# Reciprocals of softmax sums moved to ScalarE as exp(-ln), fewer k^T v bursts, and another eviction order at the first weight folds

## The chip, the cores and the metric

One core of one Trainium2 chip runs the kernel. Its engines are TensorE (PE in the profile, with its weight loads as PEld), VectorE (DVE), ScalarE (ACT), GpSimd (POOL) and SyncE (SP, which here only issues DMAs). The metric is the device time of one execution in microseconds; lower is better.

## The reference

A transformer block on x of 2048 rows and 640 columns: a linear attention with 32 heads of 20 columns, then a gated feed-forward network of width 1536. Inputs and output are bf16.

```python
x = A_x
h  = x + A(layernorm(x))
h2 = h + (gelu(ln(h) @ w_gate) * (ln(h) @ w_up)) @ w_down

# A: per head
pq, pk = q @ w_phi, k @ w_phi
phi_q = concat(softmax(pq), softmax(-pq))      # over 20 columns each
phi_k = concat(softmax(pk), softmax(-pk))
kv  = phi_k^T v ;  z = sum over rows of phi_k
o   = (phi_q kv) / (phi_q z + 1e-6)            # then @ wo
```

## The kernel before

The 2048 rows are 16 tiles of 128 rows (t = 0 to 15), with all 640 columns in the free dimension; four tiles make a block b. Nothing is left to a planner: `manual_schedule` keeps the order in which the code is written, on every engine's queue. So an instruction that waits holds all that is written behind it on the same engine.

**Folds.** w_phi is multiplied into the weights first: `fold` makes W_k w_phi and W_q w_phi in five chunks of 128 rows each. A chunk is a few matmuls into a PSUM tile `wa` (L248) and one eviction into Wk2 or Wq2, on ScalarE for the chunks listed in KA and QA (L257), else on VectorE (L259). The five W_k folds stand ahead of the main loop, the five W_q folds in its iterations 10 to 14 (FQ).

**Main loop, L494 to L534, t = 0 to 15.** One iteration does, in this order on each queue: the layernorm of tile t+6 on ScalarE (`ln_ap`, L151, up to t = 9; its transpose is a DMA that SP issues, L167); `k_tile(t)`: ten matmuls into `pk` (L296), then two exponentials on ScalarE, exp(pk) and exp(-pk), into E(t) (L340); a fold of W_q (t = 10 to 14); a burst of `kv_tile`s if KVG names t; at t = 15 the q products (`q_mm`, L396) and their exponentials (`q_exp`, L401) with the burst KVQ after the first group; `v_mm(t+3)` (L296) and its eviction `v_ev(t+3)` on ScalarE (L316) into the buffer vS of which there are NV; `k_norm(t)`.

**k_norm(t), L343.** VectorE sums E(t) over each head's 20 columns (`sk`, 64 sums a row, L347) and takes reciprocals (`rs`, L351). Then E(t) is multiplied by rs in place, in two halves (L355): the exp(-pk) half on GpSimd, the exp(pk) half on GpSimd too for the tiles in VP, else on VectorE, one iteration later (`todo`).

**k^T v bursts, L370.** `kv_tile(t)` is 32 small matmuls (L374), one for each head, with 32 columns of v as weights, all accumulating into one PSUM tile `kvp`. They run in bursts: tiles 0 and 1 in iteration 6, tiles 2 to 4 in iteration 9, tiles 5 to 8 in iteration 13, tiles 9 to 12 between q groups, tiles 13 to 15 after the loop. E has 10 buffers: E(t) overwrites E(t-10) once its `kv_tile` is done.

**PSUM.** Up to the middle of the feed-forward stage all PSUM tiles (`pk`, `pv`, `wa`, `tp`, `kvp`, `pq`) come from one pool, psG, of four buffers; a buffer is reused after its tile has been evicted. `kvp` keeps one from its first burst to the end of k^T v, and three rotate.

**After the loop**: `kv_mask` (VectorE), then attention and the feed-forward network, woven together from L831 on. None of that is touched.

Of the kernel before, what the change touches and what calls it, by code (L numbers as in the profile page):

```python
# [11 lines left out]
ACTF = mybir.ActivationFunctionType  # L12
# [5 lines left out]
def kernel(  # L18
# [12 lines left out]
    nc = tc.nc  # L31
    P = 128
    S = 2048
    D = 640
    H = 32
# [9 lines left out]
    H0 = [(P * c) // Dh for c in range(NC)]  # L45
    NH = [(P * c + P - 1) // Dh - H0[c] + 1 for c in range(NC)]
    VP = (0, 2, 4, 6, 7, 9, 11, 12)
    KA, QA = (0, 1, 4), (0, 1, 2, 3, 4)
    LQ = (7, 9, 9, 9, 10)
    FQ = (10, 11, 12, 13, 14)  # L50

    QG = ((5, 6), (0, 1), (2, 3), (4,), (7, 8), (9, 10), (11, 12), (13, 14), (15,), (16,), (17,), (18,), (19,))
    QT = (15, 15, 15, 15)
    T3 = 3

    KVG = {6: (0, 1), 9: (2, 3, 4), 13: (5, 6, 7, 8)}
    KVQ = {0: (9, 10, 11, 12)}
    VC = Dh + 1
    KC = Dh + 2
# [8 lines left out]
    SLOT = [(5 * (c // 2) + 2 * (c % 2), 3 * (c // 2) + c % 2, 2 + c % 2) for c in range(NC)]  # L68
    SL = 12
    DC = 512 - 9 * KC  # L70
    NV = 11

    x_v = A_x.rearrange("b (p t) d -> p (b t) d", t=NT)
    o_v = out.rearrange("b (p t) d -> p (b t) d", t=NT)
# [33 lines left out]
    def small(pool, shape, name, bufs=3):  # L108
        return pool.tile(shape, F32, name=name, bufs=bufs)

    def gtile(name):
        return psG.tile([P, 2, 512], F32, name=name, tag="G")
# [62 lines left out]
    p1 = p1_cm.__enter__()  # L175
    Wv = p1.tile([P, NC, D], BF16, name="Wv")
    Wk2 = p1.tile([P, NC, D], BF16, name="Wk2")

    vF = [p1.tile([P, H * VC + 11], BF16, name=f"vS{i}") for i in range(NV)]
    vS = [v[:, 0:H * VC].rearrange("p (h f) -> p h f", f=VC) for v in vF]  # L180
# [19 lines left out]
    def load_T(WT, i, *ds):  # L200

        for d in ds:
            nc.sync.dma_start_transpose(WT[:, :, d * P:(d + 1) * P], A_wqkv[d * P:(d + 1) * P, i * D:(i + 1) * D])  # L203
# [7 lines left out]
    ones = nc.const_aps.tensor(1.0, [P, 512], BF16)  # L211
    for i in range(NV):
        nc.vector.memset(vS[i][:, :, 0], 1.0)
    make_identity(nc, ident)
    nc.gpsimd.memset(hmask, 1.0)
    for c in range(NC):
# [4 lines left out]
                                compare_op=ALU.is_ge, fill=0.0, base=Dh - 1 - off, channel_multiplier=-1)  # L221
    for i in range(NV):
        nc.gpsimd.memset(vF[i][:, H * VC:], 1.0)
# [8 lines left out]
    def fold(WT, W2, quarters, ds=range(NC)):  # L232


        n, w = (2, QF) if quarters else (1, HD)
        runs = []
        for c in range(NC):
            lo, hi = H0[c] * Dh, (H0[c] + NH[c]) * Dh
            for r in range(2 * n):
                a, b = max(lo, r * w), min(hi, (r + 1) * w)  # L240
                if a < b:
                    runs.append((r // n, r, c, a, b))
        runs.sort()
        for d in ds:
            wa = gtile("wa")
            wr = wa.rearrange("p u (q x) -> p (u q) x", q=n)
            for i, (u, r, c, a, b) in enumerate(runs):
                nc.tensor.matmul(wr[:, r, a - r * w:b - r * w], lhsT=WT[:, c, d * P:(d + 1) * P],  # L248
                                 rhs=BD[:, c].rearrange("p a b -> p (a b)")[:, a - H0[c] * Dh:b - H0[c] * Dh],
                                 start=(i == 0 or runs[i - 1][0] != u),  # L250
                                 stop=(i + 1 == len(runs) or runs[i + 1][0] != u), skip_group_check=True)
            dst, src = W2[:, d, :].rearrange("p (u f) -> p u f", u=2), wr[:, :, 0:w]
            if quarters:
                dst = W2[:, d, :].rearrange("p (c r f) -> p r c f", c=NC, r=4)
                src = src.rearrange("p r (c f) -> p r c f", c=NC)
            if d in (QA if quarters else KA):
                nc.scalar.copy(dst, src)  # L257
            else:
                nc.vector.tensor_copy(dst, src)  # L259
# [19 lines left out]
    def ln_ap(t, on_act=False, on_pe=False):  # L279
        ln = (ln_act if on_act else ln_dve)(p1, "1", *lnp[t])  # L280
        if on_pe:
            lnp[t] = ln
        else:
            transpose_to(LN1T[t // 4][:, :, t % 4 * P:(t % 4 + 1) * P], ln, False)

    def ln_tp(t, on_dve=False):
        transpose_to(LN1T[t // 4][:, :, t % 4 * P:(t % 4 + 1) * P], lnp[t], True, on_dve)
# [5 lines left out]
    def proj(ps, t, W, us=(0, 1), cs=None):  # L293
        order = [(u, c) for u in us for c in range(NC)] if cs is None else [(u, c) for c in cs for u in us]
        for u, c in order:
            nc.tensor.matmul(ps[:, u, 0:HD], lhsT=lnT(t, c), rhs=W[:, c, u * HD:(u + 1) * HD],  # L296
                             start=(c == 0), stop=(c == NC - 1))
# [3 lines left out]
    def v_mm(t, us=(0, 1)):  # L301
        if 0 in us:
            pv[t] = gtile("pv")
        proj(pv[t], t, Wv, us)
# [10 lines left out]
    def v_ev(t):  # L315
        nc.scalar.activation(vS[t % NV][:, :, 1:VC].rearrange("p (u h) f -> p u h f", u=2),  # L316
                             pv[t][:, :, 0:HD].rearrange("p u (h f) -> p u h f", f=Dh), ACTF.Copy,
                             scale=lnp[t][2] if t in CT else 1.0)
# [7 lines left out]
    def k_part(t, *cs):  # L326
        if 0 in cs:
            pks[t] = gtile("pk")
        proj(pks[t], t, Wk2, cs=cs)

    def k_tile(t):
        if t in pks:
            pk = pks[t]
            k_part(t, NC - 1)
        else:
            pk = gtile("pk")
            proj(pk, t, Wk2)
        Ek[t] = ev.tile([P, 2, D], BF16, name="E", bufs=10)
        for s in range(2):
            nc.scalar.activation(Ek[t][:, s, :].rearrange("p (u f) -> p u f", u=2), pk[:, :, 0:HD],  # L340
                                 ACTF.Exp, scale=((lnp[t][2], nrstd[t]) if t in CT else (1.0, -1.0))[s])

    def k_norm(t):  # L343


        sk = small(p1, [P, 2 * H], "sk")
        nc.vector.reduce_sum(sk, Ek[t].rearrange("p s (h f) -> p (s h) f", f=Dh), axis=AX.X)  # L347
        if t - 1 in todo and t < NT - 1:
            todo.pop(t - 1)()
        rs = small(p1, [P, 2 * H], "rs")  # L350
        nc.vector.reciprocal(rs, sk)  # L351

        def mult(s, eng):
            e = Ek[t][:, s, :].rearrange("p (h f) -> p h f", f=Dh)
            eng.tensor_tensor(e, e, rs[:, s * H:(s + 1) * H, None].to_broadcast([P, H, Dh]), ALU.mult)  # L355

        mult(1, nc.gpsimd)
        if t in VP:
            mult(0, nc.gpsimd)
        elif t == NT - 1:  # L360
            todo.pop(t - 1)()
            mult(0, nc.vector)
        else:
            todo[t] = lambda: mult(0, nc.vector)

    todo = {}

    def kv_tile(t):

        E = Ek[t].rearrange("p s (h f) -> p s h f", f=Dh)  # L370
        for i in range(QH):
            for r in range(4):
                h = r * QH + i
                nc.tensor.matmul(kvp[QUAD[r], :, i * Dh:(i + 1) * Dh], lhsT=vF[t % NV][:, h * VC:h * VC + 32],  # L374
                                 rhs=E[:, :, h, :], start=(i == t == 0), stop=(t == NT - 1), skip_group_check=True)
# [23 lines left out]
    def q_exp(j, signs=(0, 1)):  # L399
        for s in signs:  # L400
            nc.scalar.activation(Eq[j][:, :, s, :], pqs[j][:, 0:len(QG[j])], ACTF.Exp, scale=(1.0, -1.0)[s])  # L401
# [66 lines left out]
    ln_st(4, act=False, between=lambda: ln_ap(3, on_pe=True))  # L468
    ln_tp(3, True)
    nc.sync.dma_start(x_sb[1][:, 2:4, :], x_v[:, 6:8, :])  # L470
    fold(WkT, Wk2, False, (0,))
    v_ev(2)
    fold(WkT, Wk2, False, (1,))
    ln_st(5, act=False, between=lambda: ln_ap(4))
    nc.sync.dma_start(x_sb[2][:, 0:2, :], x_v[:, 8:10, :])
# [18 lines left out]
    for t in range(NT):  # L494
        if t == T3:
            kvp = gtile("kvp")[:, 0, 0:2 * QF].rearrange("p (s f) -> p s f", s=2)
        late = t in (1, 4)
        if 0 < t < NT - 6 and not late:
            ln_ap(t + 6, on_act=True)
        k_tile(t)  # L500
        if t == 0:
            ln_ap(6)
            nc.sync.dma_start(x_sb[3][:, 0:2, :], x_v[:, 12:14, :])
        if t in FQ:
            fold(WqT, Wq2, True, [i for i, f in enumerate(FQ) if f == t])
        for i in KVG.get(t, ()):
            kv_tile(i)
        for j in range(len(QT)):
            if t == QT[j]:
                q_mm(j)  # L510
                q_exp(j)
                for i in KVQ.get(j, ()):
                    kv_tile(i)
        if 0 < t < NT - 3:
            v_mm(t + 3)
        if late:
            ln_ap(t + 6, on_act=True)
        if t == 1:
            nc.sync.dma_start(x_sb[3][:, 2:4, :], x_v[:, 14:16, :])
        if 0 < t < NT - 3:  # L520
            v_ev(t + 3)
        for i in ST.get(t, ()):
            ln_st(i, i + 1)
        k_norm(t)
        load_T(WqT, 0, *[i for i, f in enumerate(LQ) if f == t])
        if t == 10:
            transpose_to(LN1T[0][:, :, P:2 * P], ln_a(1), False)
        if t == 13:
            ln_ap(0, on_act=True)
        if t == 8:  # L530
            for z in KT:
                nc.gpsimd.memset(z, 0.0)
        if t == 13:
            nc.sync.dma_start(Wo, wo_v)  # L534
# [402 lines left out]
```

## Time and profile before

| | |
|---|---|
| Time, median of 3 runs | 272.33 us (272.25 to 272.48) |
| The profiled execution's own time | 272.0 us |
| Its span, first to last instruction | 270.3 us |
| Granted TensorE clock | 1.0 |
| Main loop's first burst of k^T v | 30.75 us |
| End of the last burst of k^T v | 67.1 us |
| Instructions of `sk`, mean | 16, 1.43 us each |
| Instructions of `rs`, mean | 16, 0.55 us each |

The profile is of one execution; what lies between its span and its time is start and end of the launch. In a timeline line the columns are start and duration in us, engine, source line, operation, output and inputs with their shapes, the number of instructions that the line merges, and in brackets the idle time of the engine before it with what ended it. In a group's line a bar is followed by busy time in us and the mean of one in ns, then by idle time before. Instructions of ScalarE and VectorE overlap a little at their ends, so a step from start to start is shorter than a duration.

### The profile page before, as it was taken

What the parts mean: (1) busy time and instruction counts of PE and PEld (TensorE: products, weight loads), DVE (VectorE), ACT (ScalarE), POOL (GpSimd) and SP (SyncE); (2) the same over time, 40 slices, a digit from 0 to 9 for tenths busy, and PEclk for the clock granted to TensorE, in tenths of its full rate; (3) what the DMA queues carried; (4) which work ended last, traced back from release to release, by engine and by line L of the source; (5) the groups of instructions that cost most, each with busy time, mean ns of one, the idle gap of its engine ahead of it and who ended that gap; (6) DMA issues with size and microseconds to landing.
All of it is one profiled execution on the core that took longest, in us unless ns stands there. A gap on an engine that the chain in (4) does not pass through costs nothing.

```text
span 270.3 us, 7032 instructions
## 1 busy us (share of the span) xinstructions
PE 265.5 (98%) x2851; PEld 171.7 (64%) x2867; DVE 176.4 (65%) x348; ACT 138.1 (51%) x248; POOL 99.5 (37%) x236
## 2 busy tenths in 40 slices
PE   8999999999999999999999999999999999999995
PEld 6777777764455887788755455775555476444574
DVE  5899999998876758876566783568663322333322
ACT  5769997887789675245541356321544300322100
POOL 5448988794002335376211664014561100000000
PEclk9999999999999999999999999999999999999999
DMA  7998255240678432332201224103222101000011
GB/s 192 213 203 175 54 86 100 62 127 26 233 260 232 155 101 62 41 98 51 52 24 51 49 50 51 49 2 78 78 41 52 24 24 51 24 0 0 4 49 49
DMA packets 45264, 22.10 MB, mean 82 GB/s; under 512 B 37808, under 2 KB 43184, under 8 KB 45232
## 3 DMA queue, kind: packets, MB, share of 16 engines
q1 hardware_dynamic: 44576, 21.64, 33.0%
q8 instruction: 22, 0.36, 0.6%
q10 hardware_dynamic: 656, 0.03, 0.2%
q14 instruction: 10, 0.08, 0.1%
HBM read 10.18 MB, written 2.62 MB: 47 GB/s over the span
## 4 chain that ended last, share of the span: by engine, by line
PE 87%; SPq 4%; DVE 2%; POOL 2%; DMA 2%; issue 1%; ACT 1%; ACTq 0%; POOLq 0%
PE gu L767 38%; PE pd L789 20%; PE po L707 8%; PE pq L396 8%; PE pk L296 5%; PE pv L296 4%; SPq L203 2%; PE kvp L374 2%; DMA x_sb<-in_A_x_dram 2%; PE ab L618 1%; POOL E L355 1%; DVE stats L121 1%; PE ab L585 1%; PE wa L248 1%; DVE sk L347 1%
## 5 line engine op out<-in xcount | busy, mean ns | idle before, releaser
L770 ACT ACTIVATE g<-gu 128x512 bf16<-128x512 f32 (+1 forms) x60 | 30.4, 510 | 74.0 <-PE gu L767 73.2
L773 DVE TENSOR_TENSOR GT<-gu,g 128x512 bf16<-128x512 f32 (+1 forms) x60 | 34.4, 580 | 46.6 <-PE gu L767 38.8
L767 PE MATMUL gu<-LN2T,Wg 128*128 128x512 bf16 (+1 forms) x290 | 61.3, 335 | 0.5
L767 PE MATMUL gu<-LN2T,Wu 128*128 128x512 bf16 (+1 forms) x300 | 61.8, 336 | 0.0
L789 PE MATMUL pd<-Wd,GT 128*128 128x320 bf16 (+4 forms) x396 | 53.9, 295 | 0.0
L789 PEld LDWEIGHTS <-GT 128*128 128x128 bf16 x396 | 37.6, 98 | 14.5 <-DVE GT L773 0.2
L767 PEld LDWEIGHTS <-Wu 128*128 128x128 bf16 x300 | 29.4, 98 | 22.6
L767 PEld LDWEIGHTS <-Wg 128*128 128x128 bf16 x300 | 29.0, 98 | 21.2
L296 PEld LDWEIGHTS <-LN1T 128*128 128x128 bf16 x290 | 28.0, 98 | 10.6 <-issue 0.2
L355 POOL TENSOR_TENSOR E<-E,rs 128x640 bf16<-128x640 bf16 x24 | 30.2, 1288 | 6.5 <-DVE rs L351 6.2
L791 DVE TENSOR_TENSOR y<-pd,x_sb 128x320 bf16<-128x320 f32 (+4 forms) x33 | 15.8, 480 | 24.1 <-PE pd L789 24.1
L707 PE MATMUL po<-Wo,oT 128*128 128x320 bf16 x160 | 24.5, 299 | 0.0
L296 PE MATMUL pk<-Wk,LN1T 128*128 128x320 bf16 x160 | 24.4, 299 | 0.0
L396 PE MATMUL pq<-LN1T,Wq 128*128 128x512 bf16 x94 | 22.6, 379 | 0.3
L347 DVE TENSOR_REDUCE sk<-E 128x64 f32<-128x1280 bf16 x16 | 22.9, 1430 | 0.0
L401 ACT ACTIVATE Eq<-pq 128x1024 bf16<-128x1024 f32 (+1 forms) x26 | 19.9, 832 | 2.9 <-PE pq L396 2.7
L707 PEld LDWEIGHTS <-oT 128*128 128x128 bf16 x160 | 15.6, 98 | 7.3 <-ACT oT L165 0.2
L340 ACT ACTIVATE E<-pk 128x640 bf16<-128x640 f32 x28 | 18.7, 746 | 2.7 <-PE pk L296 2.7
L296 PE MATMUL pv<-Wv,LN1T 128*128 128x320 bf16 x130 | 19.8, 299 | 0.1
L151 ACT ACTIVATE ln<-x_sb,v,rstd 128x640 bf16<-128x640 bf16 x14 | 12.9, 920 | 13.0 <-POOL v L746 12.8
L396 PEld LDWEIGHTS <-Wq 128*128 128x128 bf16 x100 | 9.4, 98 | 10.3
L682 DVE TENSOR_TENSOR tt<-AB,w 128x1280 bf16<-128x1280 f32 x10 | 15.1, 1506 | 0.4 <-POOL w L675 0.3
(120 smaller groups left out, 292.3 us busy)
## 6 DMA issues: line engine op xcount, KB each, us to landing
out_dram<-y SPq DMA_DIRECT2D x15, 160.0 KB, 1.8
x_sb<-in_A_x_dram SPq DMA_DIRECT2D x6, 320.0 KB, 3.9
Wu<-in_B_w_up_dram SPq DMA_DIRECT2D x1, 1920.0 KB, 8.8
Wg<-in_B_w_gate_dram SPq DMA_DIRECT2D x2, 768.0 KB, 6.6
Wd<-in_B_w_down_dram SPq DMA_DIRECT2D x1, 1440.0 KB
Wo<-in_A_wo_dram SPq DMA_DIRECT2D x1, 800.0 KB, 5.5
x_sb<-in_A_x_dram SPq DMA_DIRECT2D x4, 160.0 KB, 3.3
Wv<-in_A_wqkv_dram SPq DMA_DIRECT2D x2, 320.0 KB, 4.2
```

The source lines that it names most:

```text
L296: nc.tensor.matmul(ps[:, u, 0:HD], lhsT=lnT(t, c), rhs=W[:, c, u * HD:(u + 1) * HD], start=(c == 0), stop=(c == NC - 1))
L340: nc.scalar.activation(Ek[t][:, s, :].rearrange("p (u f) -> p u f", u=2), pk[:, :, 0:HD], ACTF.Exp, scale=((lnp[t][2], nrstd[t]) if t in C ...
L347: nc.vector.reduce_sum(sk, Ek[t].rearrange("p s (h f) -> p (s h) f", f=Dh), axis=AX.X)
L355: eng.tensor_tensor(e, e, rs[:, s * H:(s + 1) * H, None].to_broadcast([P, H, Dh]), ALU.mult)
L396: nc.tensor.matmul(pqs[j][:, i, :], lhsT=Wq2[:, kc, c * P:(c + 1) * P], rhs=LN1T[b][:, kc, :], start=(kc == 0), stop=(kc == NC - 1))
L401: nc.scalar.activation(Eq[j][:, :, s, :], pqs[j][:, 0:len(QG[j])], ACTF.Exp, scale=(1.0, -1.0)[s])
L707: nc.tensor.matmul(pos[u], lhsT=st[t][:, c, :], rhs=Wo[:, c, u * HD:(u + 1) * HD], start=(c == 0), stop=(c == NC - 1))
L767: nc.tensor.matmul(gu[i][:, 0:n], lhsT=W[:, c, f * P:(f + 1) * P], rhs=LN2T[b][:, c, a0:a1], start=(c == 0), stop=(c == NC - 1))
L770: nc.scalar.activation(g[:, 0:n], gu[0][:, 0:n], ACTF.Gelu_apprx_tanh)
L773: nc.vector.tensor_tensor(st[b, "g", f][:, a0:a1], gu[1][:, 0:n], g[:, 0:n], ALU.mult)
L789: nc.tensor.matmul(pd[:, 0:f1 - f0], lhsT=st[b, "g", f][:, tl * P:(tl + 1) * P], rhs=Wd[:, f, f0:f1], start=(f == 0), stop=(f == NF - 1), ...
L791: nc.vector.tensor_tensor(y[:, f0:f1], pd[:, 0:f1 - f0], x_sb[b][:, tl, f0:f1], ALU.add)
```

## The change

Four things.

- For tiles 11 to 14 (RA) the reciprocal of sk is no longer taken by VectorE. `k_norm(t)` stores sk, and `k_log(t)`, called in the next iteration straight after `k_tile(t+1)`, computes Ln of sk in place and then exp(-ln) into rs, both on ScalarE. The two multiplications follow from there (`k_div`), on the engines they had.
- The bursts at iterations 6, 9 and 13 (2, 3 and 4 tiles) become bursts at 9 and 13 (4 and 5 tiles). With the two that stay there are four: 4, 5, 4 and 3 tiles. NV goes from 11 to 12, one more buffer for v, with its memsets.
- Ahead of the loop, the eviction of v of tile 2 is written before the first W_k fold instead of after it.
- W_k's chunk 3 is evicted by ScalarE instead of VectorE (KA).

```diff
-    KA, QA = (0, 1, 4), (0, 1, 2, 3, 4)
+    KA, QA = (0, 1, 3, 4), (0, 1, 2, 3, 4)
...
+    RA = (11, 12, 13, 14)
 
-    KVG = {6: (0, 1), 9: (2, 3, 4), 13: (5, 6, 7, 8)}
+    KVG = {9: (0, 1, 2, 3), 13: (4, 5, 6, 7, 8)}
     KVQ = {0: (9, 10, 11, 12)}
...
-    NV = 11
+    NV = 12
...
         nc.vector.reduce_sum(sk, Ek[t].rearrange("p s (h f) -> p (s h) f", f=Dh), axis=AX.X)
         if t - 1 in todo and t < NT - 1:
             todo.pop(t - 1)()
+        if t in RA:
+            logs[t] = sk
+        else:
+            rs = small(p1, [P, 2 * H], "rs")
+            nc.vector.reciprocal(rs, sk)
+            k_div(t, rs)
+
+    def k_log(t):
+
+        sk = logs.pop(t)
         rs = small(p1, [P, 2 * H], "rs")
-        nc.vector.reciprocal(rs, sk)
+        nc.scalar.activation(sk, sk, ACTF.Ln)
+        nc.scalar.activation(rs, sk, ACTF.Exp, scale=-1.0)
+        k_div(t, rs)
+
+    def k_div(t, rs):
 
         def mult(s, eng):
...
-    todo = {}
+    todo, logs = {}, {}
...
     nc.sync.dma_start(x_sb[1][:, 2:4, :], x_v[:, 6:8, :])
+    v_ev(2)
     fold(WkT, Wk2, False, (0,))
-    v_ev(2)
     fold(WkT, Wk2, False, (1,))
...
         k_tile(t)
+        if t - 1 in logs:
+            k_log(t - 1)
         if t == 0:
```

## The prediction

> **What bounds the kernel now.** I read the page's busy shares and the chain that ended last, then the chain's pieces between 28 and 70 us, where the diff works, then the timeline of all engines from 50 us on, and last the groups of ScalarE with shapes kept apart.
>
> ```profile
> PE 265.5 (98%) x2851; PEld 171.7 (64%) x2867; DVE 176.4 (65%) x348; ACT 138.1 (51%) x248; POOL 99.5 (37%) x236
> PE 87%; SPq 4%; DVE 2%; POOL 2%; DMA 2%; issue 1%; ACT 1%; ACTq 0%; POOLq 0%
> ```
>
> TensorE (PE) is busy for 98% of the span and is 87% of the chain. What reaches it as idle time costs the end; what only relieves another engine is worth nothing by itself.
>
> ```profile
> 30.08 1.36 ACT E L340 x2
> 31.44 0.04 issue
> 31.48 1.52 PE pv L296 x10
> ...
> 39.79 1.04 PE kvp L374 x96
> 40.83 1.47 PE pv L296 x10
> ...
> 52.81 0.33 PE wa L248 x8
> 53.14 1.17 PE kvp L374 x128
> 54.31 1.47 PE pk L296 x10
> ```
>
> From 31.48 on the chain is all PE: a PE delay later than that is a delay of the end. The projections step by 1.36 per ten matmuls without a hole. 31.48 is the one place where the chain passes through ScalarE: v's product of tile 9 begins when E of tile 5 (30.08 + 1.36) has left its PSUM buffer.
>
> ```profile
> 49.79 1.30 ACT L340 ACTIVATE E<-pk 128x640 bf16<-128x640 f32 x2 [0.56 <-PE pk L296]
> 50.98 0.70 ACT L257 CAST Wq<-wa 128x640 bf16<-128x640 f32 x1
> 51.55 0.74 ACT L316 ACTIVATE vS<-pv 128x640 bf16<-128x640 f32 x1
> 51.57 1.47 DVE L347 TENSOR_REDUCE sk<-E 128x64 f32<-128x1280 bf16 x1
> 52.64 0.50 PE L248 MATMUL wa<-BD,WqT 128*128 128x140 bf16 x8
> 52.84 1.30 ACT L340 ACTIVATE E<-pk 128x640 bf16<-128x640 f32 x2 [0.56 <-PE pk L296]
> 53.07 1.24 PE L374 MATMUL kvp<-E,vS 128*32 128x40 bf16 x128
> 53.69 0.54 DVE L351 RECIPROCAL rs<-sk 128x64 f32<-128x64 f32 x1
> 54.16 1.42 DVE L347 TENSOR_REDUCE sk<-E 128x64 f32<-128x1280 bf16 x1
> 54.24 1.53 PE L296 MATMUL pk<-Wk,LN1T 128*128 128x320 bf16 x10
> ```
>
> This is the stage that decides. ScalarE is up to date: each E follows its pk at once (E of tile 12 at 49.79). VectorE is not: the sixteen sk rows count off as tiles 0 to 15, so 51.57 is sk of tile 11, whose E was finished at 48.04, 3.5 us earlier. VectorE shows no wait between 18 and 66 us; its backlog starts at 15.60, where its row waits for a DMA of x issued at 11.48. Nobody on PE or ScalarE waits for that backlog now: reciprocals feed only the multiplications, and those only the k^T v bursts. The last burst (66.22) comes with VectorE's last multiplication (66.21), but PE's own q row lasts to 66.29, so relief of VectorE wouldn't start it earlier.
>
> **The change, part by part.**
>
> Reciprocals. Four VectorE reciprocals go (0.55 each, stepping 0.47: some 1.9 us of VectorE). In their place ScalarE runs Ln and Exp, written behind the E of the next tile and ahead of that iteration's fold eviction and v eviction. So Ln of tile 11 stands behind E12 (ended 51.09) and ahead of the W_q eviction of tile 12 (50.98) and v of tile 15 (51.55). It needs sk of tile 11, ready at 51.57 + 1.47 = 53.04. Nothing in the diff brings that forward: its only relief of VectorE before is one W_k eviction at 13.4 to 15.1, ahead of the DMA wait at 15.60, which swallows it. ScalarE therefore waits some 2 us, and everything behind in its queue with it.
>
> Who waits for ScalarE: PSUM has four buffers and kvp holds one, so three rotate. When PE comes to the fold of tile 13 (52.64) they hold fold 12, v of 15 and pk of 13, all evicted by ScalarE behind that Ln. The first to come free is fold 12's, whichever order the pool uses.
>
> The price of Ln and Exp on 128x64 isn't in the trace; the nearest rows are these:
>
> ```profile
> L634 ACT COPY LN1T<-pd 128x176 f32<-128x176 f32 x3 | 0.9, 305 | 1.7 <-DVE y L791 1.7
> L131 ACT ACTIVATE ve<-mv,eps 128x1 f32<-128x1 f32 x2 | 0.6, 302 | 0.1
> L634 ACT COPY LN1T<-pd 128x22 f32<-128x22 f32 x3 | 0.5, 183 | 0.0
> L132 ACT ACTIVATE rstd<-ve 128x1 f32<-128x1 f32 x2 | 0.4, 204 | 0.1
> ```
>
> Between 0.18 (22 wide) and 0.31 (176 wide), 64 lies near 0.22 to 0.25; I take 0.235. The Exp needs the Ln's end: at the start of the kernel a Ln ends at 10.04 and its Exp begins at 10.08, 0.04 later. The next independent instruction starts 0.10 before an ACTIVATE's end (E12 ends 49.79 + 1.30 = 51.09, the W_q eviction starts 50.98). A pair holds ScalarE 0.235 + 0.04 + 0.235 - 0.10 = 0.41; ends 0.30 and 0.55. Handover from VectorE to ScalarE: 0.03 (mv to the Ln at 9.75) to 0.17 (rs to POOL); I take 0.10.
>
> So Ln starts 53.14, the W_q eviction 53.55, ends 54.25 (0.70). With 0.05 of handover (E to pv at 31.48) the fold of 13 starts at 54.30 instead of 52.64: 1.66 late. Ends: 54.12 and 54.51, 1.48 to 1.87.
>
> The next pairs: VectorE then does sk12 from 53.69 to 55.12 with no reciprocal between; ScalarE reaches Ln12 only at 55.9 (v15 54.12, E13 54.70 to 56.0), no wait. Ln13 falls behind E14 (57.82 to 59.11, PE late by then) and holds the eviction of fold 14, the last chunk of W_q, to 59.42-60.12; the fifth matmul of the first q group needs it at 58.17 + 1.94 = 60.11. That costs 0.06 (none to 0.21). Ln14 ends before q's first exponential has its product. POOL's multiplications start 0.5 earlier and stay in order; those of tile 12 end near 59.1, the burst comes after 61.
>
> Bursts. A burst has 0.10 ahead of its first matmul (pk slot ends 52.98, kvp at 53.07). 128 matmuls take 1.17 to the next row, 96 at the last burst 0.87: 0.29 a tile. The burst of two at tile 6 goes and one of four stands at tile 9. kvp takes its buffer when first written, so four buffers rotate until tile 9 and v9 doesn't wait for E5: from pk of tile 6 (29.29) to the next v after the burst it is now 40.76 - 29.29 = 11.47; then 7 x 1.36 + 0.10 + 1.17 = 10.79, and 0.7 is gained. The burst at tile 13 has five tiles: plus 0.29. The gain lies ahead of the wait for sk11, which is fixed by VectorE: PE arrives 0.7 earlier and waits 0.7 longer. Only the 0.29 behind it counts.
>
> First folds. v's eviction of tile 2 comes first on ScalarE, in its idle 0.66 before the W_k eviction at 11.62; v of tile 3 then finds its buffer 0.17 earlier (weight load idle 0.17). W_k chunk 3 moves from VectorE (0.80) to ScalarE (0.70), in its idle 1.01 before 15.64; without that idle it would cost 0.58. Bounds 0.1 lost to 0.17 gained, and either way absorbed by the same wait. The twelfth v buffer: a memset of 0.085 before the 0.82 that VectorE waits for x. On SP, tile 0's transpose and the Wo load behind it go out some 2.3 later: Wo lands near 65 (5.5 after issue), first needed 77.35; tile 0's transpose lands near 61, q's second group starts past 62.
>
> Sum: 1.66 + 0.29 + 0.06 = 2.0 (ends 1.8 and 2.4, the 0.29 being common). Behind tile 13 PE has no slack to give it back. The profiled execution took 272.0; 274.0. The median stands 0.33 above it: 274.3.
>
> **Rivals.**
>
> (a) The sums come early enough: not slower. VectorE's backlog holds three rows swollen beside POOL, the multiplications at 39.59 (1.29) and 46.61 (1.74) against 0.81 and the normalisation at 50.73 (0.91 against 0.45), 1.87 in all. It decides at break-even if sk11 ends by 51.1, 1.94 earlier; at 50.5 the whole burst and start gain stays: 0.17 + 0.7 - 0.29 = 0.58, so 271.75. Against it: POOL's times follow VectorE's own reciprocals, unchanged before tile 11.
>
> (b) The same wait, shorter: one of these rows falls free of POOL (0.5 to 1.4 earlier), and the end is 272.9 to 273.8.
>
> (c) The stall cools TensorE. PE would stand idle from about 51.8 to 54.3, 2.5 us, where today its longest hole after the start is below 0.5. The opening matmuls show what a cold start costs: 27 weight loads of 128 columns in 2.92, 0.108 each, against 0.056 (five transposes in 0.28, at 78.03) later. That stretch lasts from 0.8 to 4.6; half speed over as long, 3.8, adds 1.9: 276.2. For it: nothing in 270 us of work shows such a hole, so none shows that it is harmless. Against: 2.5 is shorter than the opening stretch.
> By the Trainium skill ("TensorE: Matmul & The Clock Gate", Why this matters for your kernels) PE should have no idle gaps over about 3 us, or the clock halves. By that rule 2.5 us stays just under; no run here shows it yet.
>
> Also possible in name, table loads between Ln and Exp: at 1.28 each, eight would cost ScalarE 10 us, but Ln and Exp at L131 and L132 run without one. I give it no chance of its own.
>
> **How the numbers follow.** Main case 0.80, own range 273.7 to 275.0 (the ends plus 0.2 for where sk11 falls); (b) 0.08; (a) 0.07, of it 0.05 faster by over 0.2%, 0.02 within; (c) 0.05. Below 273.4 lie (a) and half of (b), above 275.1 (c), with small tails of the main case: under 0.2 in all. 0.2%, or 0.54 us, is about what a measurement of this kernel can tell from no change. Faster, within, slower: 0.05, 0.02, 0.93.
>
> **What would show it.** Right: an idle time of some 2 us on ScalarE ahead of the first Ln, released by sk, and 2 to 2.5 us idle on PE at the fold of tile 13; four bursts, with v of tile 12 near 40; VectorE waiting for E13 afterwards. Wrong: sk of tile 11 ending before 51.5, a fold of 13 that starts on time, or matmul steps doubled after the hole.

## The result and the profile after

The changed kernel takes 274.9 us (median; 273.84 to 276.08) against 272.33 before (271.62 to 272.48): the ratio is 1.0097, with a 95% interval of 1.007 to 1.0123. Its profiled execution took 274.49, 2.49 more than the one of before. In the six executions the mean granted TensorE clock was 1.0 in two (273.84 and 274.49) and 0.993 or 0.994 in four (274.8 to 276.08); this matters below.

These are lines of the page of the changed kernel: busy time of each engine, shares of the chain that ended last, and the group of VectorE's sums.

```profile
PE 266.2 (98%) x2867; PEld 171.1 (63%) x2867; DVE 173.4 (64%) x344; ACT 140.4 (51%) x257; POOL 100.0 (37%) x237
...
PE 79%; DVE 12%; SPq 4%; issue 2%; DMA 2%; ACT 0%; POOL 0%; DVEq 0%; ACTq 0%; POOLq 0%
...
L348 DVE TENSOR_REDUCE sk<-E 128x64 f32<-128x1280 bf16 x16 | 23.1, 1443 | 2.5 <-ACT E L341 2.5
```

VectorE is busy 3.0 us less and ScalarE 2.3 us more, as the change says. But VectorE's share of the chain rose from 2% to 12%: an engine that was relieved now stands on the path. The last line shows what it does with its relief: it waits 2.5 us for E. The same group of before had no wait:

```profile
L347 DVE TENSOR_REDUCE sk<-E 128x64 f32<-128x1280 bf16 x16 | 22.9, 1430 | 0.0
```

The piece of that chain at the place of the prediction, in order of time (start, duration, engine, output, line):

```profile
51.51 1.49 DVE sk L348
52.99 0.02 issue
53.02 0.26 ACT sk L362
...
53.37 0.26 ACT rs L363
53.62 0.59 ACT Wq L258
54.21 0.04 issue
54.25 0.49 PE wa L249 x8
54.75 1.47 PE kvp L389 x160
56.21 1.47 PE pk L297 x10
```

Before, all of this stretch was PE. Now the path runs through VectorE's sum of tile 11, ScalarE's Ln and Exp of that sum, and the W_q eviction behind them, and only then back to TensorE. The same stage in the timeline of all engines:

```profile
47.09 0.51 PE L249 MATMUL wa<-BD,WqT 128*128 128x140 bf16 x8 [1.12 <-DMA WqT<-in_A_wqkv_dram]
...
53.02 0.26 ACT L362 ACTIVATE sk<-sk 128x64 f32<-128x64 f32 x1 [1.37 <-DVE sk L348]
...
53.53 0.67 ACT L258 CAST Wq<-wa 128x640 bf16<-128x640 f32 x1
...
54.25 0.49 PE L249 MATMUL wa<-BD,WqT 128*128 128x140 bf16 x8 [0.89 <-ACT Wq L258]
54.26 0.34 PEld L249 LDWEIGHTS <-WqT 128*128 128x128 bf16 x7 [1.09 <-issue]
...
54.68 1.54 PE L389 MATMUL kvp<-E,vS 128*32 128x40 bf16 x160
...
56.03 1.49 DVE L348 TENSOR_REDUCE sk<-E 128x64 f32<-128x1280 bf16 x1 [0.92 <-ACT E L341]
56.15 1.53 PE L297 MATMUL pk<-Wk,LN1T 128*128 128x320 bf16 x10
...
59.21 2.47 PE L411 MATMUL pq<-LN1T,Wq 128*128 128x512 bf16 x10
...
61.60 1.13 PE L389 MATMUL kvp<-E,vS 128*32 128x40 bf16 x119
...
63.08 0.23 PE L389 MATMUL kvp<-E,vS 128*32 128x40 bf16 x9 [0.35 <-issue]
...
63.24 2.98 PE L411 MATMUL pq<-LN1T,Wq 128*128 128x512 bf16 x13
```

These are two later rows of before:

```profile
59.56 1.23 PE L374 MATMUL kvp<-E,vS 128*32 128x40 bf16 x128
...
60.72 5.57 PE L396 MATMUL pq<-LN1T,Wq 128*128 128x512 bf16 x24
```

Set against the same rows of before, the loss builds up in four steps:

| row of TensorE | before | after | late |
|---|---|---|---|
| fold of tile 13 | 52.64 | 54.25 | 1.61 |
| pk of tile 14 | 54.24 | 56.15 | 1.91 |
| burst between q groups | 59.56 | 61.60 | 2.04 |
| q products behind that burst | 60.72 | 63.24 | 2.52 |

The first step is ScalarE's wait, the second the fifth tile of the burst, the third the first q group. The fourth was not in the prediction: the burst between the q groups stops for 0.35 us, 119 matmuls in, at no wait of any other engine ("issue"). The idle time at 47.09 is a chunk of W_q^T that landed 5.2 us after its issue (2.9 to 3.4 before); it ate lead that TensorE would have lost anyway at 54.25, so the hole there is 0.89 us and not 2.0.

### The profile page after: what moved, and what is told of

Same layout as the page of the kernel before. It is cut to its first block, busy times and chain, and to the rows that moved or that the text cites. A ratio compares the mean times of both kernels' runs of the same rounds, so it can differ in the third digit from the quotient of the medians.

```text
span 272.8 us, 7048 instructions
## 1 busy us (share of the span) xinstructions
PE 266.2 (98%) x2867; PEld 171.1 (63%) x2867; DVE 173.4 (64%) x344; ACT 140.4 (51%) x257; POOL 100.0 (37%) x237
## 4 chain that ended last, share of the span: by engine, by line
PE 79%; DVE 12%; SPq 4%; issue 2%; DMA 2%; ACT 0%; POOL 0%; DVEq 0%; ACTq 0%; POOLq 0%
PE gu L784 38%; PE pd L806 19%; PE pq L411 8%; PE po L724 8%; DVE sk L348 6%; DVE stats L122 2%; SPq L204 2%; DVE rs L355 2%; DMA x_sb<-in_A_x_dram 2%; PE ab L635 1%; PE kvp L389 1%; PE pk L297 1%; PE ab L602 1%; DVE mv L126 0%; DVE E L370 0%
```

## The experiments

"Before" below is the kernel before, run beside the experiments on the same chip: its medians were 272.87 (runs 1 to 4), 272.88 (runs 5 to 8), 272.68 (runs 9 to 11) and 272.72 (run 12), each group on another chip, and its 99 executions there span 271.93 to 274.43. A profile is of one execution. All diffs are against the changed kernel unless the text says otherwise.

**1. The reciprocals alone.** Bursts, v buffers and the order at the start as before.

```diff
-    KA, QA = (0, 1, 3, 4), (0, 1, 2, 3, 4)
+    KA, QA = (0, 1, 4), (0, 1, 2, 3, 4)
...
-    KVG = {9: (0, 1, 2, 3), 13: (4, 5, 6, 7, 8)}
+    KVG = {6: (0, 1), 9: (2, 3, 4), 13: (5, 6, 7, 8)}
...
-    NV = 12
+    NV = 11
...
+    fold(WkT, Wk2, False, (0,))
     v_ev(2)
-    fold(WkT, Wk2, False, (0,))
```

> The kernel before with the first part of the change alone: reciprocals of tiles 11 to 14 by ScalarE; bursts, buffers and start as before. Theory (ScalarE waits for the sum of tile 11 and TensorE waits for the fold eviction behind it): the fold of tile 13 starts near 54.3 instead of 52.64, 1.66 late, plus 0.06 at the first q group, so about 274.1 us; ScalarE idle about 1.9 us ahead of the first Ln. Rival (the regrouped bursts make the loss): 272.3 us. Rival (the work of Ln and Exp, not the wait): four pairs of 0.4 us spread over four tiles, with no single hole on TensorE, 272.5 to 273.5 us.

Measured: 274.73 (274.43 to 275.23), ratio 1.008 (1.0052 to 1.0108), 1.86 more than before. The timeline of this kernel:

```profile
53.45 0.26 ACT L362 ACTIVATE sk<-sk 128x64 f32<-128x64 f32 x1 [2.06 <-DVE sk L348]
...
54.68 0.49 PE L249 MATMUL wa<-BD,WqT 128*128 128x140 bf16 x8 [1.58 <-ACT Wq L258]
```

The wait and the hole stand at the same instructions as in the changed kernel, without any change to bursts or start. The fold of 13 came at 54.68 and not near 54.3 because the sum itself ended later in this execution, at 53.41. The reciprocals alone make a loss of the size of the whole: 1.86, where the changed kernel lost 2.57 at first and 1.47 in run 5.

**2. All but the reciprocals.**

```diff
-    RA = (11, 12, 13, 14)
+    RA = ()
```

> The changed kernel without its first part: all reciprocals on VectorE; four bursts, twelve v buffers and the new start stay. Theory: no ScalarE wait, TensorE keeps its lead: 0.7 (no burst at tile 6) minus 0.29 (fifth tile at 13) plus up to 0.17 (start) gained, 271.8 to 271.9 us. If the transposed load of W_q's second chunk lands as late as in the changed kernel's profile (47.0 us), the fold of tile 11 waits for it and the lead is lost: 272.3 to 273.1 us. Rival (the bursts make the loss): 274 us or more.

Measured: 272.41 (271.96 to 273.93), ratio 0.9991 (0.9974 to 1.0009): not told from no change. Five executions lie at 271.96 to 272.27 and five at 272.54 to 273.93 (those of before beside it at 271.97 to 273.42), and the profiled one, 273.08, is of the second five. Its timeline shows the stop inside the burst again, longer:

```profile
59.66 1.13 PE L389 MATMUL kvp<-E,vS 128*32 128x40 bf16 x119
61.67 0.23 PE L389 MATMUL kvp<-E,vS 128*32 128x40 bf16 x9 [0.88 <-issue]
```

So that stop needs no reciprocal on ScalarE. It is not what took the expected lead, though: the burst starts at 59.66 against 59.56 before, so the lead was gone when the stop came. What became of it stands with run 8.

**3. One pair, one iteration later.** Only tile 11 goes to ScalarE, and its Ln is written two iterations after its sum, when the sum has long been there.

```diff
-    RA = (11, 12, 13, 14)
+    RA = (11,)
...
-        if t - 1 in logs:
-            k_log(t - 1)
+        if t - 2 in logs:
+            k_log(t - 2)
```

> The changed kernel with only tile 11's reciprocal on ScalarE, and its Ln and Exp one iteration later, behind the E of tile 13 instead of tile 12. Theory: the sum (53.0) is then ready before ScalarE gets there (about 53.3 to 54.1), so no wait, and 0.4 us of ScalarE work lies in its slack: 271.8 to 272.1 us, as without any ScalarE reciprocal. Rival (the Ln and Exp themselves, or POOL's later multiplication of tile 11, cost): 272.5 us or more.

Measured: 273.74 (273.55 to 274.03), ratio 1.0037 (1.0022 to 1.0052). My number missed. ScalarE's part went as I said: the fold of 13 started on time, at 52.24. But the timeline shows another hole, in the burst between the q groups:

```profile
56.29 10.47 POOL L370 TENSOR_TENSOR E<-E,rs 128x640 bf16<-128x640 bf16 x7 [3.22 <-DVE rs L355]
...
59.56 0.67 PE L389 MATMUL kvp<-E,vS 128*32 128x40 bf16 x64
...
61.88 0.66 PE L389 MATMUL kvp<-E,vS 128*32 128x40 bf16 x64 [1.65 <-POOL E L370]
```

Moving the Ln moved tile 11's multiplications on GpSimd behind those of tile 12, which wait for VectorE's reciprocal. GpSimd stood idle for 3.22 us and delivered late what the burst needs. The edit cured one wait and made another, the one that the expectation names as its rival.

**4. The sum a little earlier.** VectorE's layernorm of q's tile 1, which stands ahead of the sum of tile 11, is written two iterations later.

```diff
-        if t == 10:
+        if t == 12:
             transpose_to(LN1T[0][:, :, P:2 * P], ln_a(1), False)
```

> The changed kernel with VectorE's normalisation of tile 1 (0.91 us, stepping 0.84, at 50.68, just ahead of the sum of tile 11) written two iterations later. Theory: the sum of tile 11 ends 0.84 earlier, near 52.15, the fold of tile 13 starts near 53.4 instead of 54.25, and the time falls by 0.84 against the changed kernel's 274.9, to about 274.1 us. Rival (the wait doesn't set the end): no change, 274.9 us. A hole of TensorE that is shorter should also leave the granted clock at 1.0 if the drop to 0.994 in some runs of the changed kernel comes from the hole.

Measured: 273.74 (273.4 to 274.08), ratio 1.0033 (1.0021 to 1.0044), 0.87 more than before. The sum ended at 52.42 instead of 52.98, and the timeline follows it:

```profile
52.45 0.26 ACT L362 ACTIVATE sk<-sk 128x64 f32<-128x64 f32 x1 [1.80 <-DVE sk L348]
...
53.69 0.49 PE L249 MATMUL wa<-BD,WqT 128*128 128x140 bf16 x8 [1.32 <-ACT Wq L258]
```

The fold of 13 came at 53.69 instead of 54.25: 0.56 for 0.56 of the sum. I had expected 0.84, and one profile doesn't say what the edit was worth, since in two executions of the changed kernel the sum ended at 52.98 and 53.55 (run 5). But the fold follows the sum in all of them: in the profiles of the changed kernel and of runs 1, 4, 5 and 6 the sum ends between 52.42 and 53.55, and the fold of 13 starts 1.26 or 1.27 later each time. What VectorE did to the sum, TensorE got.

**5. The changed kernel again.** No edit; for its spread.

> The changed kernel again, beside the kernel before on the same chip. Theory (the wait for the sum of tile 11): 2.0 to 2.6 us above the kernel before. In its first runs four of six executions showed a granted clock of 0.994 and 274.8 to 276.1 us, two a clock of 1.0 and 273.8 to 274.5. If TensorE's idle time ahead of tile 13's fold cools it, runs at 0.994 appear here too; if that was that chip's own matter, the clock stays at 0.999 to 1.0 and all runs stay within 0.5 us of each other.

Measured: 274.35 (274.12 to 276.04), ratio 1.0063 (1.004 to 1.0087), 1.47 more than before where I had expected 2.0 to 2.6. Why the loss is smaller here isn't known. Six of ten executions lie at 274.12 to 274.39 with a clock of 1.0; four lie at 275.39, 275.71, 275.8 and 276.04, all with 0.994. The profiled one is of the four. Its timeline:

```profile
53.58 0.26 ACT L362 ACTIVATE sk<-sk 128x64 f32<-128x64 f32 x1 [2.68 <-DVE sk L348]
...
54.81 0.49 PE L249 MATMUL wa<-BD,WqT 128*128 128x140 bf16 x8 [2.20 <-ACT Wq L258]
...
56.72 2.81 PE L297 MATMUL pk<-Wk,LN1T 128*128 128x320 bf16 x10
```

and its stretches of 5 us (stretch, then length and busy time of PE, PEld, DVE, ACT and POOL, the granted clock, the DMA share and GB/s):

```profile
50.00:55.00 5.00, 2.80 (x25) 1.95 (x23) 4.90 (x6) 2.23 (x6) 4.02 (x4) 1.00 0.17 33
55.00:60.00 5.00, 5.00 (x189) 3.64 (x186) 2.16 (x2) 3.79 (x8) 4.25 (x4) 0.66 0.08 17
```

The sum came 0.57 later here and the lead was not eaten by a DMA, so the hole was 2.2 us, 2.4 between weight loads. Then ten matmuls of pk took 2.81 instead of 1.53. The trace's clock record has half speed from 55.95 to 59.36, 3.41 us.

**6. One pair, where the change puts it.**

```diff
-    RA = (11, 12, 13, 14)
+    RA = (11,)
```

> The changed kernel with only tile 11's reciprocal on ScalarE, its Ln and Exp where the change puts them, behind the E of tile 12 and ahead of the fold eviction. Theory: this one wait is nearly the whole loss: fold of tile 13 near 54.3 as with four, so the four's time less what the later pairs cost (0.46 at the first q group): 0.3 to 0.5 us below the changed kernel. Rival (each of the four reciprocals costs its share): a quarter of the loss, about 0.6 us above the kernel before.

Measured: 274.6 (274.3 to 275.31), ratio 1.0065 (1.0046 to 1.0084), 1.72 more than before. One pair costs as much as four (1.47 in run 5, beside it). In its timeline Ln waits 2.10 and the fold of 13 starts at 54.54 after a hole of 1.62. So there is no cost per pair, and my expectation that a single pair would be some tenths cheaper was wrong too.

**7. The same pair, behind the evictions.** Ln and Exp of tile 11 are written behind the W_q eviction and v's eviction.

```diff
-    RA = (11, 12, 13, 14)
+    RA = (11,)
...
-        if t - 1 in logs:
-            k_log(t - 1)
...
             v_ev(t + 3)
+        if t - 1 in logs:
+            k_log(t - 1)
```

> As the kernel with one reciprocal on ScalarE, but the Ln and Exp of tile 11 written two places later on ScalarE: behind the fold eviction of tile 12 and the v eviction of tile 15, ahead of the E of tile 13. Theory: ScalarE waits for the sum all the same (about 1.6 us), but only the E of tile 13 stands behind the wait, and its PSUM buffer is needed again only by the fold of tile 14 near 55.0, about when that E is done (54.8 to 55.0): TensorE loses 0 to 0.3 us, and the time is 0.1 to 0.5 us below the kernel before. Rival (the wait of ScalarE itself, wherever it stands, sets the end): as with the Ln ahead of the fold eviction, 1.5 us or more above the kernel before.

Measured: 272.54 (272.15 to 273.31), ratio 0.9992 (0.9973 to 1.001). The loss is gone; a gain isn't shown. ScalarE runs the same instructions and still waits 1.49 us for the sum, and the fold of 13 starts on time:

```profile
52.34 0.50 PE L249 MATMUL wa<-BD,WqT 128*128 128x140 bf16 x8
...
53.47 0.26 ACT L362 ACTIVATE sk<-sk 128x64 f32<-128x64 f32 x1 [1.49 <-DVE sk L348]
```

The loss was neither the work of Ln and Exp nor a wait on ScalarE by itself, but the two evictions queued behind that wait.

**8. The bursts alone.** The kernel before with the new KVG and NV.

```diff
-    KVG = {6: (0, 1), 9: (2, 3, 4), 13: (5, 6, 7, 8)}
+    KVG = {9: (0, 1, 2, 3), 13: (4, 5, 6, 7, 8)}
...
-    NV = 11
+    NV = 12
```

> The kernel before with the regrouped bursts and the twelfth v buffer alone. Theory: 0.7 gained ahead of tile 10, 0.29 given back at tile 13: 0.4 us below the kernel before. Rival (fewer, longer bursts save only the 0.10 switch each): 0.1 below, which isn't told from no change.

Measured: 273.41 (272.3 to 277.04); without the three executions at 276.42 to 277.04, whose clock was 0.994, the ratio is 1.0005 (0.9985 to 1.0025). The gain that I expected didn't show. The profile is of one of the three:

```profile
59.95 1.13 PE L374 MATMUL kvp<-E,vS 128*32 128x40 bf16 x119
...
63.36 0.25 PE L374 MATMUL kvp<-E,vS 128*32 128x40 bf16 x9 [2.28 <-issue]
```

The stop is at the same matmul as in run 2, now 2.28 long, and the clock record has half speed from 63.42 to 66.84, again 3.41 us. No Ln, no wait for a sum is in this kernel.

The stop isn't the only reason for the missing gain: both terms of the bursts were mis-sized. From pk of tile 6 to v of tile 12 TensorE takes 10.92 us with the new bursts (29.84 to 40.76 here, 29.56 to 40.48 in run 2, 29.10 to 40.02 in the changed kernel) against 11.47 before: 0.55 gained, not 0.7. From the fold of 13 to pk of 14 it takes 2.00 here and 1.99 in run 2 against 1.60 before: 0.4 lost, not 0.29. That leaves 0.15, which these runs can't tell from nothing. In this profile it was lost too, because pk of tile 6 came 0.55 later than before.

**9. The order at the start alone.** The kernel before with the new KA and v's eviction of tile 2 ahead of the first fold.

> The kernel before with the new start alone: v eviction of tile 2 ahead of the first W_k fold, W_k chunk 3 evicted by ScalarE. Theory: TensorE is 0.17 to 0.4 us earlier up to tile 6, and loses it at v of tile 9, which waits for E of tile 5, an engine chain of VectorE, GpSimd and ScalarE that the start doesn't move: no change, within 0.2 us of the kernel before. Rival (the start's gain reaches the end): 0.2 to 0.4 us below.

Measured: 272.46 (272.04 to 273.98), ratio 0.9996 (0.9982 to 1.0011). This doesn't decide: the interval reaches from 0.5 below to 0.3 above and holds both no change and the rival's 0.2 to 0.4. In the profile the lead went elsewhere than I had said: a v product starts 0.11 earlier (12.26 against 12.37), but the W_k fold at 15.16 is already 0.04 later than before.

**10. and 11. The instruction stream shifted by six matmuls.** If the stop comes where TensorE's instructions are fetched, six more matmuls at the start move the burst against it. Run 10 is run 8, run 11 is run 2, each with this edit:

```diff
-    warm(*[512] * 2, *[P] * 28)
+    warm(*[P] * 36)
```

> The regrouped bursts alone, with the two opening warm-up matmuls of 512 columns replaced by eight of 128, which take the same time and put six more weight loads and matmuls ahead of everything else. Theory (the holes of 0.4 to 2.4 us near the 120th matmul of the burst between q groups are TensorE running out of fetched instructions: a 16 KB block is fetched when a block boundary is passed, here after the first matmuls of the first q group, and a burst uses a block up in 1.1 us): the boundary is passed six matmuls earlier, in the rows ahead of q, more than 1 us more for the fetch; no hole there, no execution at 276 us or more, and a median near 272.4 us, 0.4 below the kernel before. Rival (the holes don't depend on the place in the instruction stream): some executions at 276 to 277 us as before, median near 273.3.

> The changed kernel without ScalarE reciprocals, with the same eight warm-up matmuls instead of two. Theory: as above, the lead of 0.4 to 0.6 us reaches the end in all executions: 272.0 to 272.4 us where the kernel before takes 272.9. Rival: spread from 272.0 to 273.9 as without the shift.

Measured: run 10 274.0 (272.35 to 275.81), ratio 1.004 (1.0013 to 1.0067); run 11 272.66 (272.14 to 275.81), ratio 1.0012 (0.999 to 1.0033). The stop did not vanish, so the expected times are wrong. But its place in the burst moved as the idea has it. The timeline of run 10:

```profile
60.31 1.08 PE L374 MATMUL kvp<-E,vS 128*32 128x40 bf16 x113
...
63.31 0.27 PE L374 MATMUL kvp<-E,vS 128*32 128x40 bf16 x15 [1.92 <-issue]
```

It now comes after 113 matmuls instead of 119: at the same place in TensorE's stream, ahead of the 863rd weight load of the trace. A smaller stop in run 10 (0.20 in a row of pk at 57.39) is ahead of the 735th, 128 pairs of weight load and matmul earlier. The trace has a queue for instructions, which moves packets of 16 KB, 22 in the span; one packet runs ahead of each stop. These are the records of that queue beside the weight loads (us; load 734 is the last one ahead of the earlier place, and the stop is the step from load 862 to load 863, about 0.01 in a burst that runs through):

```
kernel     load 734   instruction packet   load 863   stop    Wo's bytes mostly
before       57.31      57.88 to 59.21      60.55     0.01     59.0 to 61.3
after        59.21      60.21 to 61.60      63.08     0.54     61.3 to 63.4
run 2        57.41      59.40 to 60.33      61.67     1.07     58.5 to 61.0
run 8        57.70      61.01 to 62.07      63.36     2.47     59.0 to 61.4
run 10       56.89      60.87 to 61.91      63.31     2.10     59.0 to 61.4
run 11       56.62      57.95 to 59.42      60.77     0.18     58.5 to 61.0
run 12       56.98      58.74 to 59.69      61.13     0.20     before 52
```

After a stop the work goes on 1.3 to 1.5 us behind the packet's end, and in no profile of this case does load 863 come less than 1.29 behind it. That TensorE waits for this packet is inferred from these times; the trace doesn't say it. In the profiles without a long stop the packet starts at most 1.8 us after load 734; in runs 2, 8 and 10 it starts 2.0, 3.3 and 4.0 after it, while Wo's bytes move or are nearly through. The short stop of the changed kernel is not of that kind: its packet starts 1.0 after load 734, ahead of Wo's bytes, and takes 1.39. The burst runs through 128 pairs in 1.2 to 1.4 us, so it has little time to spare for its next packet.

All profiles with such a stop (run 6 has 0.19) have the regrouped bursts; before and runs 1 and 9, with the old ones, have none, but neither do runs 3, 4, 5 and 7. Whether the old bursts are safe from it isn't shown.

**12. Wo's load out of the way.** Run 10, with the 800 KB load of Wo issued in iteration 9 instead of 13.

```diff
-        if t == 13:
+        if t == 9:
```

> The regrouped bursts with the eight warm-up matmuls, as in the run whose median was 274.0 us (7 of 12 executions above 273.9), and the 800 KB load of Wo issued in iteration 9 (near 46.6 us) instead of 13 (56.8). There the hole of 2.0 us near 61.3 ended 1.4 us after an instruction block that was fetched at 60.87 instead of near 58, while Wo's bytes ran from 59 to 61. Theory (the block waits behind Wo's load): with Wo over by 52, the block comes near 58, the hole in the burst between q groups is gone, no execution is above 273.6, median near 272.4 us. Rival (the block is late for another reason): holes and median as before, 273.5 us or more.

Measured: 272.91 (272.14 to 273.42), ratio 1.0001 (0.9986 to 1.0017). In run 10 seven of twelve executions lay above 273.9 (3 of the 99 of before); here, on another chip, none lies above 273.42. The burst runs through but for 0.2 us:

```profile
46.73 0.51 PE L248 MATMUL wa<-BD,WqT 128*128 128x140 bf16 x8 [0.50 <-DMA WqT<-in_A_wqkv_dram]
...
60.05 1.36 PE L374 MATMUL kvp<-E,vS 128*32 128x40 bf16 x128
```

So the long stops go with Wo's load. The median is still not below before: Wo now collides with the transposes of W_q, and TensorE waits 0.50 at 46.73. In what way Wo's load delays the packet isn't settled; each of these profiles is one execution.

None of the versions is told apart from the kernel before as faster: the lowest, runs 2, 7 and 9, have intervals that hold 1.

## Why the prediction was right, and where it was off

- **ScalarE waits for the sum of tile 11: right, and shown.** The sum was put at 53.04 and ended at 52.98. Runs 1 and 6 give the loss with the wait, run 7 takes away what is queued behind the wait and the loss goes, and in five profiles the fold starts 1.26 to 1.27 behind the sum's end. The idle times that I named as signs, some 2 us on ScalarE and 2 to 2.5 on TensorE, were 1.37 and 0.89 in the first profile, where the late chunk had held TensorE for 1.12 before; in run 5 they were 2.68 and 2.20.
- **The fold of 13, 1.66 late: measured 1.61** (54.25 against 54.30). Two terms were off and nearly cancelled. The pair held ScalarE 0.51 (53.02 to 53.53), not 0.41: each instruction took 0.26, not 0.235, and the Exp started 0.09 after the Ln's end, not 0.04. The handover from VectorE took 0.04, not 0.10. By the Trainium skill ("ScalarE: Activation LUTs", What ACT_TABLE_LOAD costs) an ACTIVATE with immediate scale and bias takes 186 ns and 0.833 ns per column, which for 64 columns makes an estimate of 0.24; the trace has 0.26.
- **The bursts behind tile 13, 0.29: right in the changed kernel,** 0.30 between the first two steps of the table above. In runs 2 and 8, with no hole ahead of it, the same step is 0.4.
- **The first q group, 0.06: within its bounds (none to 0.21).** The fold's chunk was late for its fifth matmul (0.46 idle between weight loads, of which 0.13 reached the next step). The term is mis-sized by 0.07.
- **No gain from the bursts' lead ahead of tile 13: right in the whole kernel,** where VectorE's sum sets the end. In that profile a late chunk of W_q^T took it even earlier. The bursts' part of that lead was 0.55 and not 0.7 (run 8), which changes nothing here.
- **What the sum left out: the stop in the burst between q groups.** It is 0.48 of the 2.49 in the profiled execution, and nearly all of the difference between 274.0 predicted for it and 274.49. The sum has no term for it. It appears without reciprocals too (runs 2 and 8), so it is no part of the wait for the sum.
- **Rival (c), the clock, was given 0.05 and happened in many executions.** Mean clocks of 0.994 in four of ten executions of run 5, and in four of six of the first measurement, go with 1.0 to 1.9 us more than their neighbours in run 5 (275.39 to 276.04 against 274.12 to 274.39). (c) priced this at 1.9, from a slow stretch of 3.8 us; it was 3.41. My argument against it, that 2.5 us is shorter than the opening stretch of 3.8, was the wrong yardstick: a hole of 2.2 was enough in the profile of run 5, one of 2.28 in run 8, and (c)'s own sign, matmul steps doubled after the hole, stands in run 5. It fits that the first median is 274.9 and not lower, since four of its six executions had it. Whether in those it followed the hole at the fold, as (c) has it, or the stop in the burst, as in run 8, isn't known.
- **Rivals (a) and (b)** didn't occur in either profile of the changed kernel: the sum of tile 11 ended at 52.98 and, in run 5, at 53.55.

So the mechanism and its main term are right, with a small term missing and a rare case that is not rare. That 274.3 also lies among the executions at full clock (274.12 to 274.49, but for one at 273.84) is luck in part: six of these eight are run 5's, where the kernel before took 272.88 and the loss was only 1.24 to 1.51, not the 2.0 of the sum.

## What to carry to other kernels

Before moving an operation to an engine that has time, look at the instant when its input is ready and at what is queued behind it in written order: here 0.5 us of work cost 1.6, and the same work two instructions later cost nothing that could be measured. Moving it later again changes the order on every queue that the moved step feeds (GpSimd in run 3), so follow all of them. And where TensorE is the bound, a hole of 2 us is not only 2 us: ask whether the clock holds.

## What the runs showed of the hardware

- **The clock can fall after a hole of 2.2 us, if the hole lies badly.** The profiles of runs 1, 3, 4 and 6 have holes of TensorE of 1.3 to 1.7 us, and all 31 executions of these kernels had a clock of 0.999 or above. Holes of 2.2 and 2.3 us, in the profiles of runs 5 and 8, were followed by half speed for 3.41 us; one of 1.92 (run 10) was not. The slowest execution of run 11 (275.81) had 0.994 too, but no profile. By the Trainium skill ("TensorE: Matmul & The Clock Gate", Part 1 and Why this matters for your kernels) the clock falls after an idle window of about 3.4 us, and idle gaps should stay under some 3 us. The hole needed here was shorter.
- **The changes lie on a grid of 3.41 us.** Counted from the first rise to full clock in the same execution, at 4.74 and 5.40 us, the falls and returns come 15 and 16 steps later in run 5 (55.95 and 59.36) and 17 and 18 in run 8 (63.42 and 66.84). Each of the two holes lay wholly inside the one step ahead of the fall, in which TensorE was busy for 1.21 and 1.13 of the 3.41 us, almost only with the small matmuls of a k^T v burst (32 columns of weights each; in run 5 also eight of a fold). The next least busy steps in the profiles that record the clock, 1.83 us in run 1 and 1.85 in run 10, were followed by no fall; in run 10 the stop lay across the border of two steps (61.75). So it seems to be the idle share of a step that counts and not the hole's length. The first rise comes at 3.64 to 6.53 us in these profiles, so the same hole can fall into one step or across two; that this is why four of ten executions of run 5 were hit isn't shown. Whether small matmuls count as less work wasn't tried.
- **TensorE seems to run out of instructions.** A packet of 16 KB, as much as 128 pairs of weight load and matmul use up, took 0.9 to 1.5 us in the profiles of the table, and a burst of small matmuls goes through 128 pairs as fast. TensorE stood still for up to 2.28 us at a fixed place of its stream, with no semaphore in sight. Six more instruction pairs ahead moved the stop by six matmuls in the burst and did not remove it; with the 800 KB load issued elsewhere 0.2 us of it was left.
